# A scheduled attention and gated MLP kernel: first tile's x in two halves, four tiles gated by Silu, new priorities

## The chip, the cores and the metric

The kernel runs on one core of one Trainium2 chip. The core has five engines that work side by side, each through its own list of instructions in order: TensorE (PE, with its weight loads shown as PEld), VectorE (DVE), ScalarE (ACT), GpSimd (POOL) and SyncE (SP), which here only issues transfers. Sixteen DMA engines carry the transfers. The metric is device time in microseconds of one execution; the median of several runs is compared.

## What is computed

One sequence of 2048 tokens of width 448 is normalised. One branch is attention with 16 heads of width 28, in which a token sees eight tokens: itself and seven earlier ones, two apart. The other branch is an MLP of width 1792 with Gelu. The output is x plus the attention result times Silu of the MLP result. All arrays are bf16.

```python
xn = _layernorm(x)
q, k, v = split(xn @ wqkv)                     # 16 heads of 28
idx = pos[:, None] - 2 * arange(8)[None, :]    # masked where negative
s = (softmax(q . k[idx] * 28**-0.5) . v[idx]) @ wo
g = silu(gelu(xn @ w1 + b1) @ w2 + b2)
return x + s * g
```

## The kernel before

The tokens are split into even and odd ones, so that the dilated window becomes a plain window of eight neighbours; the 2048 positions are then cut into 16 tiles of 128 and 4 chunks of 512.

For each tile, `stats` (line 432) loads mean and variance with two DVE instructions (statistics, line 434, and aggregation, line 439), `rstds` (line 444) takes the square root on ACT and the reciprocal on DVE for the first four tiles (on POOL for the others), and `norm` (line 467) writes the normalised tile `xn` on DVE (line 469) and doubles its last 64 columns (line 474, POOL for the first four tiles). The first four tiles are transposed on PE (line 484) and copied to `xnT` (line 330 on DVE, 328 on ACT); the other twelve are transposed by DMA from SP (`dma_T`, line 389).

From `xnT` come three products. `qk_rows` (line 569) and `vproj` (line 592) give q, k and v of a tile; `first_batch` (line 542) does it for the first two tiles, weight part by weight part as the weights land, and `pair` (line 508) for two tiles or two outputs at a time, with the upper and the lower 64 rows of the array doing different work. q and k are copied to `qk_tok` and transposed by DMA to `qkT`; v goes to memory (`v_hbm`) and comes back as windows. `ff1` (line 645) gives the hidden layer, with Gelu on ACT (line 649), and `ff2` (line 677, for the last two tiles line 699) the MLP's output.

Attention goes in nine visits of up to 228 positions: scores on PE (line 744), exponential on ACT (line 753), mask on DVE (line 759), values on PE (line 773), and then on DVE two transposes, a reciprocal and a product (lines 782 to 796) that write `oT`. `final` (line 827) multiplies `oT` by wo (line 835, or 843 for the last two tiles).

The gate is in two functions. `gate` (line 712) takes the MLP output y, computes t = tanh(y/2) on ACT (line 723) and (t+1)y on DVE (line 727). `gated` (line 848) multiplies the attention result by half of that (line 850), adds x (line 856) and issues the output from SP (line 860). The last tile is cut into 336 and 112 columns (`parts`, line 660).

The order of the work is not written out. Every step is a task in `_Plan`: an engine (or several to choose from), an estimated cost, the tasks it needs, the buffers it takes and gives back, and a priority from the tables `PRIO` and `LATER`, moved by `NUDGE` for single tasks. `run` (line 99) walks through time by these estimates and, among the tasks of an engine that can start at about the same moment, takes the one with the highest priority. `emit` then writes each engine's instructions in that order. So a changed estimate or priority moves instructions on every engine, and at run time each engine follows its list and waits where an input is late.

A transfer (`dma`, line 369) is two tasks: the issue on SP, ACT or POOL, and a stretch on one modelled "DMA" engine with a rate and a tail until it has landed. At the start, x of tile 0 goes out from SP and x of tile 1 from ACT (lines 407 and 408), then from SP two of the three parts of wqkv, x of tiles 2 and 3 together, the third part and the two tails, then half of w1, x of tiles 4 to 7 and the other half. Until the first tile is there, PE runs warm-up matmuls on constants (line 343).

Of the kernel before, what the change touches and what calls it, by code (L numbers as in the profile page):

```python
# [10 lines left out]
ALU = mybir.AluOpType  # L11
# [164 lines left out]
def kernel(  # L176
# [82 lines left out]
    def ring(name, n, shape, dt=BF16, fifo=False):  # L259
# [24 lines left out]
        "project": (213.5, 84.5, 145, 57.5,),  # L284
        "project2": (61, 74.5, 113.5, -640,),
        "values": (199.5, -20, 128, 6,),
        "attn": (784, 1451, 452, 363, 27.5, 240.5, 361.5, 160.5, 204.5,),
        "ff1": (198.5, 215, 158, 71.5, 146.5, 194, 121, 197.5, 124, 116, 171.5, 143, 137, 144.5,
            114.5, 194, 150.5, 78.5, -21, 12, 47, 112.5, 51.5, 61.5, 93.5, 59.5, 175, 137,),
        "gelu": (5, 143.5, 52.5, 123.5,),  # L290
        "ff2": (805.5, -34.5, 231, 114.5, -2.5, 89, -623.5, 135, 208.5, 180.5, -39.5, 104, -4, 131,
            -80.5, -689,),
        "final": (-141.5, 2, -11, -16.5, 187, -2, 125, 203, -49.5, 65.5, -59.5, 162.5, -51, 134,
            6.5, 220.5,),
        "norm": (131, 11, 219.5, 294, 190, 208.5, 173, -1.5, 189, 173.5, 166.5, 159, 150.5, -11.5,
            127, 56,),
        "loads": (2.5, 106.5, -29, 61, -61,),
        "stats": (49, 32, 205.5, 205.5, 55, 91.5, -4.5, 56, 70.5, 178.5, 31, 101.5, -704, 2.5, 161,
            70.5,),
        "turn_x": (198, 4.5, 200, 12.5, 20.5, 38.5, 81, 163, 190.5, 214.5, 8.5, -3, 72, 153.5,  # L300
            72.5, 162.5,),
        "turn_qk": (-12.5, 15, 13, 198, 91, 58, -98.5, 69, 181.5, 168, 69.5, -36, 142, 100, 88,
            80.5,),
        "move_v": (19.5, -58, -99, 107.5, 62, 44, 64.5, 3, 68,),
        "store_v": (55.5, 68.5, -38.5, -16, 175.5, 53, 3.5, 13.5, 115.5, -7, 113, 144.5, 69, 170.5,
            147.5, 61.5,),
        "spread": (120, 175.5, 70.5, 58.5, 20, 222, 105.5, 24, 126,),
# [12 lines left out]
    def act(n):  # L320
        return 0.15 + n / 1130.0
# [19 lines left out]
    for i in range(48):  # L341
        def fn(k, n=512 if i < 10 else P):
            nc.tensor.matmul(buf(p_b, k)[:, :n], ones[:, :P], ones[:, :n], start=True, stop=True)  # L343
        t_warm = plan.add("PE", 0.427 if i < 10 else 0.107, fn, [t_warm], 1000 if i < 12 else -1000, take=(p_b,), limit=8.0)
        t_warm.give = ((p_b, t_warm, 0),)
# [23 lines left out]
    def dma(eng, dst, src, kb, prio, deps=(), issue=0.45, rate=350.0, tail=1.7):  # L369
# [5 lines left out]
        a = plan.add(eng, issue, fn, [t_on] + list(deps), prio)  # L375
        return plan.add("DMA", kb / rate, lambda _: None, [a], prio, tail=tail)
# [19 lines left out]
    def load_x(t0, n, prio, eng="SP", deps=()):  # L396
        d = dma(eng, x_sb[:, t0:t0 + n, :],
                rows(x_half, t0 * P, n * P).rearrange("(t p) d -> p t d", p=P), 112 * n, prio, deps,
                rate=250.0 if t0 < 2 * TPC else 230.0, tail=1.6 if t0 < 2 else 1.7)
        for t in range(t0, t0 + n):  # L400
            t_x[t] = d
# [5 lines left out]
    load_x(0, 1, 300, "SP")  # L407
    load_x(1, 1, 300, "ACT")
    t_w = []

    def load_w(kt, prio):
# [609 lines left out]
```

## Time and profile before

| What | Value |
|---|---|
| Median of 3 runs | 153.47 us (153.23 to 154.29) |
| The profiled execution | 153.43 us |
| Its span, from the first to the last instruction | 151.7 us |
| PE matmuls from the first warm-up to the last product | 0.84 to 147.68 us |
| HBM read and written | 9.42 MB and 3.94 MB |
| Table loads on ACT | 6, of 1.28 us each |

The profile shows one execution. "Busy" is the time in which an engine worked on an instruction; a share is of the span. The chain of work that ended last is followed back from the last instruction, at each step to what released it. A wait is put down to the event that came last. In a timeline, a row gives its start, its busy time, the engine and the line of the kernel, what is written and read, how many instructions are merged, and in brackets the idle time before it and what ended that. In the DMA issues, the last number is the time from issue to landing.

### The profile page before, as it was taken

The page shows a single profiled execution, that of the slowest core. Times are in us where ns is not written, and L with a number is a line of the kernel's source. Part 1 is how long each engine was busy: PE and PEld are TensorE (multiplying, and loading weights), DVE is VectorE, ACT ScalarE, POOL GpSimd, SP SyncE. Part 2 cuts the span into 40 slices and gives each one's busy share as a digit, 9 for nine tenths or more (in the row PEclk, how much of TensorE's full clock was granted, in tenths as well). Part 3 has the DMA queues.
Part 4 walks back from the last instruction along what each step waited for, and adds up shares of the span by engine and source line. Part 5 has one row for each costly group of instructions (what it writes and reads, how often), then busy time and mean ns, then how long its engine had stood idle before and what let it go on. Part 6 is the DMA issues. An engine that isn't in the chain of part 4 may idle for free.

```text
span 151.7 us, 5225 instructions
## 1 busy us (share of the span) xinstructions
PE 146.6 (97%) x2169; PEld 79.7 (53%) x2169; DVE 118.7 (78%) x288; ACT 90.5 (60%) x160; POOL 24.9 (16%) x62
## 2 busy tenths in 40 slices
PE   7999999999999999999999999999999999999990
PEld 2457555555567555556555554445566444554560
DVE  3786850624996997799998998889898978997972
ACT  3234969368796959658444457967396497602030
POOL 7435540100046900231201000000000000000000
PEclk9999999999999999999999999999999999999999
DMA  5999985499987973699945516222020000001221
GB/s 158 315 297 318 175 233 123 41 172 338 250 187 194 212 188 77 133 185 210 184 131 130 140 57 133 78 73 62 12 65 6 0 0 4 4 0 61 90 68 31
DMA packets 36983, 19.47 MB, mean 128 GB/s; under 512 B 24840, under 2 KB 35919, under 8 KB 36959
## 3 DMA queue, kind: packets, MB, share of 16 engines
q1 hardware_dynamic: 35774, 16.40, 47.4%
q0 software_dynamic: 1040, 2.62, 6.9%
q8 instruction: 17, 0.28, 0.7%
q10 hardware_dynamic: 144, 0.11, 0.3%
q14 instruction: 8, 0.06, 0.1%
HBM read 9.42 MB, written 3.94 MB: 88 GB/s over the span
## 4 chain that ended last, share of the span: by engine, by line
PE 95%; DVE 2%; ACT 0%; issue 0%; DVEq 0%; ACTq 0%
PE bank L645 28%; PE bank L677 25%; PE bank L569 14%; PE bank L592 7%; PE bank L835 7%; PE bank L773 4%; PE bank L699 3%; PE bank L343 3%; PE bank L744 2%; PE bank L484 1%; DVE sg L850 1%; DVE w_in L727 1%; PE bank L843 0%; DVE qk_tok L330 0%; ACT t L723 0%
## 5 line engine op out<-in xcount | busy, mean ns | idle before, releaser
L645 PE MATMUL bank<-xnT,w 64*128 64x512 bf16 x392 | 44.3, 376 | 0.0
L677 PE MATMUL bank<-w,h 64*128 64x448 bf16 x392 | 40.4, 349 | 0.0
L649 ACT ACTIVATE h<-bank,b 128x512 bf16<-128x512 f32 x56 | 34.0, 688 | 9.7 <-PE bank L645 9.3
L645 PEld LDWEIGHTS <-w 64*128 64x128 bf16 x392 | 20.4, 94 | 20.4
L677 PEld LDWEIGHTS <-h 64*128 64x128 bf16 x392 | 19.2, 94 | 16.0
L569 PE MATMUL bank<-w_in,xnT 64*128 64x448 bf16 (+1 forms) x212 | 25.1, 349 | 0.1
L753 ACT ACTIVATE E<-bank 128x456 bf16<-128x456 f32 (+1 forms) x36 | 16.8, 557 | 9.3 <-PE bank L744 9.3
L328 ACT CAST qk_tok<-bank 128x448 bf16<-128x448 f32 x23 | 11.5, 540 | 9.9 <-PE bank L569 8.5
L723 ACT ACTIVATE t<-y 128x448 f32<-128x448 f32 x15 | 8.6, 586 | 14.5 <-DVE y L717 14.5
L569 PEld LDWEIGHTS <-xnT 64*128 64x128 bf16 (+1 forms) x212 | 11.7, 94 | 9.4 <-DVE xnT L330 0.3
L782 DVE STREAM_TRANSPOSE dt<-bank 128x480 f32<-128x480 f32 (+1 forms) x18 | 12.1, 674 | 2.8 <-PE bank L773 2.8
L592 PE MATMUL bank<-w_in,xnT 64*128 64x448 bf16 (+1 forms) x106 | 13.5, 349 | 0.1
L791 DVE STREAM_TRANSPOSE dt<-rd 128x480 f32<-128x480 f32 (+1 forms) x18 | 12.1, 675 | 0.6
L835 PE MATMUL bank<-wo,oT 64*128 64x448 bf16 x112 | 12.4, 349 | 0.0
L434 DVE BATCH_NORM_STATS2 st<-x_sb 128x6 f32<-128x448 bf16 x16 | 9.6, 604 | 3.3 <-DMA x_sb<-in_A_x_dram 3.3
L759 DVE TENSOR_TENSOR E<-E,m_gen 128x456 bf16<-128x456 bf16 (+1 forms) x32 | 11.1, 387 | 1.3 <-ACT E L753 1.3
L796 DVE TENSOR_TENSOR oT<-bank,dt 128x456 bf16<-128x456 f32 (+1 forms) x18 | 11.4, 631 | 0.6
L330 DVE CAST qk_tok<-bank 128x448 bf16<-128x448 f32 x9 | 5.4, 618 | 7.8 <-ACT h L649 5.5
L717 DVE TENSOR_TENSOR y<-bank,b 128x448 f32<-128x448 f32 x15 | 8.9, 618 | 1.6 <-PE bank L677 1.6
L381 POOL DMA_DIRECT2D v_hbm<-v_tok x11 | 6.3, 572 | 21.3 <-PE bank L592 10.0
L592 PEld LDWEIGHTS <-xnT 64*128 64x128 bf16 (+1 forms) x106 | 6.0, 94 | 4.5 <-issue 0.3
L835 PEld LDWEIGHTS <-oT 64*128 64x128 bf16 x112 | 5.5, 94 | 5.1
(72 smaller groups left out, 143.7 us busy)
## 6 DMA issues: line engine op xcount, KB each, us to landing
out_dram<-o SPq DMA_DIRECT2D x15, 112.0 KB, 1.7
v<-v_hbm SPq DMA_DIRECT2D x13, 128.0 KB, 3.2
v_hbm<-v_tok POOLq DMA_DIRECT2D x11, 128.0 KB, 3.6
w<-in_B_w_dram SPq DMA_DIRECT2D x2, 672.0 KB, 7.5
x_sb<-in_A_x_dram SPq DMA_DIRECT2D x3, 448.0 KB, 6.9
w_in<-in_A_wqkv_dram SPq DMA_DIRECT2D x3, 336.0 KB, 4.4
w<-in_B_w_dram SPq DMA_DIRECT2D x2, 448.0 KB, 5.3
w<-in_B_w_dram SPq DMA_DIRECT2D x2, 336.0 KB, 6.5
```

The lines of the kernel that those rows point to most:

```text
L328: nc.scalar.copy(o, i)
L569: return nc.tensor.matmul(ps[:, :D], xnT[r, kt, cs], w, start=start, stop=stop)
L592: return nc.tensor.matmul(ps[:, :D], xnT[r, kt, k0:k0 + P], w, start=start, stop=stop)
L645: return nc.tensor.matmul(ps[:], w1[r, kt, ms], xnT[r, kt, cs], start=start, stop=stop)
L649: nc.scalar.activation(buf(p_h, own, i)[:], buf(p_b, own, i)[:], ACT.Gelu_apprx_tanh, bias=b1[:, mt:mt + 1])
L677: return nc.tensor.matmul(ps[:, :D], buf(*h_at[(c, mt)])[r, cs], w2[r, mt, :], start=start, stop=stop)
L753: nc.scalar.activation(buf(p_E, k)[:, :8 * n], buf(p_b, a, at + i)[:, :8 * n], ACT.Exp, scale=SCALE)
L759: nc.vector.tensor_tensor(out=E, in0=E, in1=m[:, :, :, :n].rearrange("p i g q -> p (i g) q"), op=ALU.mult)
L782: nc.vector.transpose(buf(p_dt, k)[:, :32 * m], buf(p_b, po, i)[:, :32 * m])
L791: nc.vector.transpose(buf(p_dt, d)[:, :32 * m].rearrange("p (b c) -> p b c", c=32), buf(p_rd, r)[:, :m].unsqueeze(2).to_broadcast((P, m, 32)))
L796: nc.vector.tensor_tensor(out=oT[:, a::2, q:q + 4 * n1], in0=buf(p_b, po, i)[:, :n].rearrange("p (l q) -> p l q", l=2), in1=buf(p_dt, d)[: ...
L835: return nc.tensor.matmul(ps[:, :D], oT[r, kt, t * P:(t + 1) * P], wo[r, kt, :], start=start, stop=stop)
```

## The change

There are four parts.

1. The start. Tile 0's x is loaded as two halves of 64 rows, one from SP and one from ACT; tile 1's x follows from ACT as a second issue. x of tiles 2 and 3 are two loads, the second behind the third part of wqkv. Loads without inputs are put in turn for the planner: on each issuing engine, and in their data. The planner's rates and tails of the transfers are new numbers. One of the ten long warm-up matmuls is now a short one.
2. Tile 0's norm stands ahead of tile 1's aggregation: `t_st[1]` gets it as an input.
3. The last four tiles (12 to 15) are gated by Silu on ACT, which writes the gate at once; the DVE step (t+1)y falls away for them, and `gated` multiplies without the factor one half. For the last tile, the sum may go to DVE or POOL and the output's issue to SP or ACT, as the planner chooses.
4. All priorities in `NUDGE`, `PRIO` and `LATER` are new, so that the planner gives a new order on every engine.

```diff
 NUDGE = {
-    82: 164, 83: 221, 88: -17, 98: 114, 148: -76, 155: 52, 210: 248, 309: -202, 522: -191, 633: 96,
-    635: 30, 656: -230, 898: 200, 985: 15,
+    76: -245, 137: -86, 141: -177, 146: -165, 158: -142, 176: 37, 178: -31, 263: -236, 298: 162, 301: 180,
...
-    LATER = {"swap": 102.5, "qk": -548.5, "v": 174.5, "gelu": 131.5, "exp": 44, "mask": -436, "pv": 158.5, "recip": 165.5, "os": 191, "y": 231, "tanh": -35.5, "g": 111.5, "sg": 40, "o": 208.5}
+    LATER = {"swap": 52.5, "qk": -1428, "v": -156.5, "gelu": 55.5, "exp": 90, "mask": -2112, "pv": 17, "recip": 91.5, "os": 93, "y": -7, "tanh": 127, "g": 168.5, "sg": 168.5, "o": 552.5}
...
-        def fn(k, n=512 if i < 10 else P):
+        def fn(k, n=512 if i < 9 else P):
...
-        a = plan.add(eng, issue, fn, [t_on] + list(deps), prio)
-        return plan.add("DMA", kb / rate, lambda _: None, [a], prio, tail=tail)
+        ahead = [] if deps else in_turn
+        a = plan.add(eng, issue, fn, [t_on] + list(deps) + [k for k, _ in ahead if k.eng == (eng,)][-1:], prio)
+        d = plan.add("DMA", kb / rate, lambda _: None, [a] + [k for _, k in ahead][-1:], prio, tail=tail)
+        if kb > 50 and not deps:
+            in_turn.append((a, d))
+        return d
...
-    load_x(0, 1, 300, "SP")
-    load_x(1, 1, 300, "ACT")
+    t_x[0] = [dma(e, x_sb[r:r + 64, 0, :], x_half[0, r:r + 64, :], 56, 300, rate=262.0, tail=1.4) for e, r in (("SP", 0), ("ACT", 64))]
+    load_x(1, 1, 299.5, "ACT", tail=1.4)
...
-    load_w(0, 299)
-    load_w(1, 298)
-    load_x(2, 2, 297, "SP")
-    load_w(2, 296)
+    load_w(0, 299, 0.85)
+    load_w(1, 298, 1.4)
+    load_x(2, 1, 297, "SP", tail=1.45)
+    load_w(2, 296, 1.45)
+    load_x(3, 1, 295.5, "SP", tail=1.4)
...
         a = plan.add("DVE", 0.40, f1, [t_rs[t]], prio if t >= TPC else 390 - t, take=(p_xn,))
+
+        if not t:
+            t_st[1].deps.append(a)
...
+        if t >= NT - TPC:
+            def f5(k):
+                nc.scalar.activation(buf(p_g, k)[:, :n], buf(pool, y, at)[:, :n], ACT.Silu)
+            t_g[t].append(plan.add("ACT", act(n), f5, after, prio + LATER["tanh"], take=(p_g,), give=held, table=("silu",)))
+            return
...
-            nc.vector.scalar_tensor_tensor(out=buf(p_sg, k)[:, :n], in0=buf(p_b, own, i)[:, :n], scalar=0.5,
-                                           in1=buf(p_g, g)[:, :n], op0=ALU.mult, op1=ALU.mult)
+            ps, by, o = buf(p_b, own, i)[:, :n], buf(p_g, g)[:, :n], buf(p_sg, k)[:, :n]
+            if t >= NT - TPC:
+                (nc.gpsimd if k.on == "POOL" else nc.vector).tensor_tensor(out=o, in0=ps, in1=by, op=ALU.mult)
+            else:
+                nc.vector.scalar_tensor_tensor(out=o, in0=ps, scalar=0.5, in1=by, op0=ALU.mult, op1=ALU.mult)
...
-        o = plan.add(("DVE", "POOL") if n == LAST else "DVE", (dve(n, 2), 0.1 + n * 0.0024) if n == LAST else dve(n, 2), f3, [s], prio + LATER["o"], take=(p_o,), give=((p_sg, s, 0),))
-
-        def f4(_):
-            nc.sync.dma_start(rows(o_half, t * P, P)[:, cs], buf(p_o, o)[:, :n])
-        q = plan.add("SP", 0.55, f4, [o], 50)
+        o = plan.add(("DVE", "POOL") if last else "DVE", (dve(n, 2), 0.1 + n * 0.0024) if last else dve(n, 2), f3, [s], prio + LATER["o"], take=(p_o,), give=((p_sg, s, 0),))
+
+        def f4(k):
+            (nc.scalar if k.on == "ACT" else nc.sync).dma_start(rows(o_half, t * P, P)[:, cs], buf(p_o, o)[:, :n])
+        q = plan.add(("SP", "ACT") if last else "SP", (0.35, 0.4) if last else 0.55, f4, [o], 50)
```

More of the change, by code (lines that the diff above doesn't have):

```diff
@@ L302 @@
[L302 to L307, printed above, removed]
+        "project": (110, 23, 95, 1.5,),
+        "project2": (61.5, 77.5, 2.5, -908.5,),
+        "values": (84, 64.5, 13, -255.5,),
@@ L435, in stats @@
         prio = PRIO["stats"][t] if t >= TPC else 380 - 2 * t
-        k = plan.add("DVE", 0.61, f1, [t_x[t]], prio, take=(p_st,))
+        k = plan.add("DVE", 0.63, f1, t_x[t], prio, take=(p_st,))
         def f2(_):
@@ L484, in f3 @@
                     nc.tensor.transpose(tp[:, kt, :], xn[:, kt * P:(kt + 1) * P], ident[:])
-            halves.append(plan.add("PE", 0.13 if t else 0.22, f3, [twice if i else a, t_ident] + halves, 400 - t, take=() if i else (p_b,),
-                                   give=((p_xn, a, 0),) if i else (), tail=0.15))
+            halves.append(plan.add("PE", 0.13 if t else 0.16, f3, [twice if i else a, t_ident] + halves, 400 - t, take=() if i else (p_b,),
+                                   give=((p_xn, a, 0),) if i else (), tail=0.12))
         b = halves[0]
@@ L720, in gate @@
         after = [a, y]
+        if t >= NT - TPC:
[3 more added lines that the diff above has]
+            return
         def f3(k):
             nc.scalar.activation(buf(p_t, k)[:, :n], buf(pool, y, at)[:, :n], ACT.Tanh, scale=0.5)
-        th = plan.add("ACT", act(n), f3, after, prio + LATER["tanh"], take=(p_t,), table=("exp", "gelu"))
+        th = plan.add("ACT", act(n), f3, after, prio + LATER["tanh"], take=(p_t,), table=("exp", "gelu", "silu"))
         def f4(k):
@@ L872, in load_w1 @@
         cs = slice(i * F // 2, (i + 1) * F // 2)
[L873 to L874 removed]
+        t_w1.append([dma("SP", w1[:, 0:3, cs], ktiles(B_w1[0:KF, cs]), 672, prio, deps, rate=262.0, tail=1.3)]
+                    + [dma("SP", w1[64 * i:64 * i + 64, 3, cs], B_w1[KF:D, cs], 112, prio, deps, rate=262.0, tail=1.3) for i in range(2)])
     load_w1(0, 91, [])
```

65 lines of the change are left out of this document (34 added, 31 removed), and 2 rows, old and new, of the table NUDGE.

## The prediction

> **What bounds the kernel now.** I read the busy shares and the chain of the page first, then the chain in order of time, then the timelines of the first 14 us and the last 14 us, and last the waits and the DMA issues. One execution is the yardstick throughout: the profiled one, 153.43 us with a span of 151.7, so 1.73 us lie around the span; the median of the runs, 153.47, is 0.04 above it.
>
> ```profile
> PE 146.6 (97%) x2169; PEld 79.7 (53%) x2169; DVE 118.7 (78%) x288; ACT 90.5 (60%) x160; POOL 24.9 (16%) x62
> ...
> PE 95%; DVE 2%; ACT 0%; issue 0%; DVEq 0%; ACTq 0%
> ```
>
> TensorE carries 95% of the chain. What is left to gain is small: the time before its first real matmul, its few waits, and the tail behind its last matmul.
>
> ```profile
> 6.11 0.30 DVE xnT L330
> 6.41 0.05 issue
> 6.46 0.36 PE bank L569
> ...
> 39.46 2.68 PE bank L569 x28
> 42.14 0.61 DVE qk_tok L330
> 42.76 0.04 issue
> 42.80 2.80 PE bank L592 x27
> ```
>
> In this chain, the first projection (L569) starts at 6.46, and one wait in the body shows: PE stands from 42.14 to 42.80 for a qk_tok copy, 0.66 us. To see the rest I sum the work by its rows: 392 ff1 matmuls x 0.108 (9.07 for 84) = 42.3; 392 ff2 x 0.0946 (2.65 for 28) = 37.1; q, k, v 300 x 0.0946 + 18 full ones x 0.189 = 31.8; wo 112 x 0.0946 = 10.6; nine score visits x 0.42 = 3.8; nine value visits x 0.72 = 6.5; the last two tiles 7.2; transposes 0.9. Together 140.2. From 6.46 to the end of the last matmul, 147.68, are 141.2 us. So PE loses 1.0 us there: 0.66 in that wait and 0.34 elsewhere, nearly all of it between 10.1 and 11.5, where tiles 2 and 3 come in.
>
> ```profile
> 3.35 0.63 DVE L434 BATCH_NORM_STATS2 st<-x_sb 128x6 f32<-128x448 bf16 x1 [1.43 <-DMA x_sb<-in_A_x_dram]
> 4.11 0.59 DVE L434 BATCH_NORM_STATS2 st<-x_sb 128x6 f32<-128x448 bf16 x1
> 5.00 0.40 DVE L469 TENSOR_SCALAR xn<-x_sb,mv,rstd 128x448 bf16<-128x448 bf16 x1
> 9.69 0.46 SPq L371 DMA_DIRECT2D v_hbm<-zero  x1
> ...
> 138.26 1.11 ACT L723 ACTIVATE t<-y 128x448 f32<-128x448 f32 x2 [6.26 <-DVE y L717]
> ...
> 146.28 0.45 ACT L723 ACTIVATE t<-bank 128x336 f32<-128x336 f32 x1 [1.62 <-PE bank L699]
> 146.76 0.76 DVE L727 SCALAR_TENSOR_TENSOR w_in<-t,bank 128x336 bf16<-128x336 f32 x2
> 147.62 0.28 DVE L850 SCALAR_TENSOR_TENSOR sg<-bank,w_in 128x112 bf16<-128x112 f32 x1
> 147.93 0.22 DVE L856 TENSOR_TENSOR o<-x_sb,sg 128x112 bf16<-128x112 bf16 x1
> 148.07 0.50 DVE L850 SCALAR_TENSOR_TENSOR sg<-bank,w_in 128x336 bf16<-128x336 f32 x1
> 148.60 0.33 DVE L856 TENSOR_TENSOR o<-x_sb,sg 128x336 bf16<-128x336 bf16 x1
> ```
>
> At the start, tile 0's statistics wait for its x until 3.35, tile 1's statistics (4.11) run ahead of tile 0's norm (5.00 to 5.40), and everything up to 6.46 follows from that norm: 1.06 us of transposes, the doubled columns on POOL, and the copy. At the end, DVE runs without a break from 146.76 to 148.93; PE is done at 147.68.
>
> ```profile
> x_sb<-in_A_x_dram ACTq DMA_DIRECT2D x1, 112.0 KB, 2.3
> x_sb<-in_A_x_dram SPq DMA_DIRECT2D x1, 112.0 KB, 2.5
> 2.00:3.00 1.00, 1.00 (x4) 0.37 (x3) 0.00 (x0) 0.69 (x2) 1.00 (x2) 1.00 1.00 312
> ```
>
> The two x tiles land 2.3 and 2.5 us after issue, side by side; the last number of the third line is what the DMA engines moved in that microsecond, 312 GB/s.
>
> **Start.** Today 224 KB are under way at once. With halves of tile 0 on both queues and tile 1 second on ACT's queue, 112 KB come first; 112 KB less at 312 GB/s is 0.36 us, so x lands near 2.95 instead of 3.30. Tile 1, issued one ACT issue (0.38) later, then lands at about 3.7 (336 KB ahead of or beside it, by the same rate), just as tile 0's statistics end (3.80). The order of the changed kernel has statistics 0, aggregation 0, statistics 1, reciprocal 0, norm 0, and only then aggregation 1. So norm 0 stands at 4.58 to 4.98, 0.42 earlier. What the added wait holds back is aggregation 1 and, behind the first xnT copy, norm 1, which ends near 6.6; PE wants it at 6.7, after three matmuls of tile 0, so it is covered by 0.1. If tile 1 lands at 4.2 (1.2 plus the 3.0 of the quickest w_in), statistics 1 block DVE and norm 0 gains 0.02. PE can take no more than 0.44: its warm-up (nine instead of ten of 0.427, then six short ones) ends at 5.01 instead of 5.45. I take 0.35 of the span 0.02 to 0.44, near the upper end since the rate row is the closest. The second issue on ACT stands ahead of its table load (1.28), which then ends at 2.9, before the first square root (3.9).
>
> **First batch.** Tile 3's x is now an issue of its own behind w_in's third part; SP issues eight loads for seven, so the tails go out 0.45 later and w1 and x 4 to 7 up to 0.6 later. The bytes ahead of the tails are the same. The v_hbm issue at 9.69 waited 0.9 us for the last of them, so they land at about 9.65; PE, 0.35 earlier, wants them at 9.6: 0 to 0.1 of wait. Norm 3 ends near 10.45 by its chain (x3 at about 8.4, then statistics, root, reciprocal, norm), and PE wants it at 10.5. Of today's 0.34 us I let 0.1 go (ends 0 and 0.34).
>
> **The body.** The new priorities reorder all engines, but the work on PE is the same except for one warm-up. What changes is who waits. The wait at 42.14 belongs to the old order: scores there follow the projections whose copies were behind eight statistics on DVE. In the new order 28 ff2 matmuls (2.65 us) stand ahead of the first scores and 56 and 14 behind: minus 0.66. Against it, I put PE's new order beside DVE's and ACT's by the rows from 48 to 92 us: six hand-overs have less than 0.3 us to spare (copies of q and k before the fourth scores, oT before three ff2 or wo groups, the exponentials before the third value visit, oT before chunk 2's first ff1). Each costs between nothing and 0.66, the longest wait of this kind in the trace; I take 0.4 for all six (ends 0 and 1.2). DVE's load there, 25.3 us of rows in 28 us, is no higher than now (27 us from 64 to 91 with under 1 idle), so it does not become the bound.
>
> **Silu and the tail.** Four tiles lose the tanh and the (t+1)y step: five DVE instructions, 0.62 x 3 + 0.50 + 0.27 = 2.6 us, go. ACT gets Silu for tanh, and a seventh table load. No Silu is in the trace; I take tanh's rows (0.58 and 0.45; the Gelu's 0.69 for 512 columns is the upper end, hardly more per column). The load stands behind the last Gelu with no wait, in the 6.26 us in which ACT was idle; without that cover it costs 1.28. Behind the last tile, sg 112 waits for its Silu (146.95 + 0.26 = 147.21) instead of two DVE steps (147.53), and the last four steps start 0.3 earlier, until sg 336 meets the end of PE. I take 0.27 (ends 0.2 and 0.30). Both last outputs stay on SP in the order built, so their 1.4 and 1.6 us are as now.
>
> **Sum.** -0.35 - 0.10 - 0.66 + 0.40 - 0.27 = -0.98: 153.43 becomes 152.45; with the 0.04 to the median, 152.5 us.
>
> **A rule weighed.** The row first: x of tile 0 takes 2.5 us beside tile 1's. The Trainium skill, DMA: Bandwidth & Descriptors (Rules for kernel authors), says of two transfers to disjoint partition halves not to bother, since both spread over the same 16 engines. By that the halves bring nothing in themselves, and what I count comes from tile 1's bytes moving behind; the sum by the rule alone is that of the third case below. The nearest row speaks for a gain, as the two tiles landed at nearly the same time though issued from two queues.
>
> **The rivals.** Clean: the first batch and the hand-overs cost nothing. -0.44 - 0.34 - 0.66 - 0.30 = -1.74: 151.7. For it speaks that the old order has one visible wait in 90 us; against it the six narrow places.
>
> No earlier start: halves and tile 1 get in each other's way, norm 0 stays near 5.00, the batch too. -0.66 + 0.40 - 0.27 = -0.53: 152.9.
>
> Slower, by the transposed x of tiles 4 to 7: today four of them go out in a row from 19.81, 1.25 us each, and land 2.6 us later. In the new SP order two more v_hbm stores and a qkT transpose stand ahead of the last two, and the stores wait for ACT copies behind the first two Gelus. By the rows (qkT 1.34, 2.06, 2.62) the third leaves at 24.1 and lands at 26.7; PE wants it at 27.5. From 0.8 us of slip PE waits, and from 1.8 the kernel is slower than before. A landing of 5.0, the longest of xnT, gives +1.6: 154.1; three qkT at the longest row, 3.56, give +4.6 - 0.8: 156.3. Against it: the landings at that time were 2.5 to 3.6.
>
> A later clock: PE's 512-column matmuls ran at 0.427 until about 4.7, 3.9 us after its start, and at twice the rate after. With one warm-up less the rise may come 3.9 us later, at 8.6; 2.5 us of the first batch would run at half rate, +1.25: 153.7. The Trainium skill, TensorE: Matmul & The Clock Gate (What's actually happening), ties the rise to time, a window of about 3.4 us, and not to a count of matmuls; the one profile agrees, and so the lost warm-up should not matter.
>
> **How the numbers follow.** Forecast 0.50, clean 0.22, no earlier start 0.13, late transposes 0.10, later clock 0.05. Within 1%, which a measurement of this kernel can about tell from no change, is 151.9 to 155.0. Faster: the clean case, 0.22. Slower: half of the late transposes, 0.05. Same: 0.73. The range 151.6 to 154.2 takes in all but the late transposes and the edge of the clean case.
>
> **What would show it.** First L569 (now at another line) near 6.1 and norm 0 ahead of aggregation 1; statistics 0 near 3.0. No wait of PE before the first scores. PE's last matmul near 147.0 and DVE's last step about 0.98 behind it. Seven table loads, the last ahead of 138. I am wrong if PE waits for xnT near 27, if the hand-overs from 62 to 92 cost over 1 us, or if statistics 0 still start at 3.3.

## The result, and the profile after

The changed kernel takes 161.94 us (median of four runs, 159.84 to 163.5) against 153.47: slower, the ratio is 1.050 with an interval of 1.039 to 1.061. The forecast was 152.5, the range 151.6 to 154.2. The profiled execution below is the slowest of the four, 163.5 us with a span of 161.8; the kernel before has a span of 151.7. Of the experiments, medians and ranges are given over all runs of a kernel, while ratios leave out runs over 1.5% above its fastest.

The busy shares, the slices of TensorE and its granted clock, and the chain, from the page of the changed kernel:

```profile
PE 149.5 (92%) x2168; PEld 77.1 (48%) x2168; DVE 112.5 (70%) x274; ACT 98.4 (61%) x170; POOL 22.6 (14%) x58
...
PE   7999999999809999999999967999999999999990
...
PEclk9999999999965999999999999999999999999999
...
PE 75%; DMA 12%; DVE 5%; SPq 3%; ACT 2%; issue 1%; POOL 0%; POOLq 0%; DVEq 0%; ACTq 0%
```

TensorE fell from 95% of the chain to 75%, and DMA transfers now hold 12%; one load of x alone holds 7% of the span. One slice is empty (the 0, near 46), and in it and the next one the clock row reads 6 and 5. Another dent is at 93 to 101 (6, 7). The chain in order of time around the empty slice:

```profile
33.46 11.05 DMA x_sb<-in_A_x_dram
44.51 0.02 issue
44.54 0.64 DVE st L442
...
47.45 0.19 DVE mv L447
47.64 0.09 issue
47.73 0.30 POOL sd L464
48.04 0.04 issue
48.08 0.03 POOLq L536
48.11 0.05 issue
48.15 1.46 PE bank L656 x6
49.62 1.49 PE bank L580 x8
51.11 1.28 PE bank L656 x6
52.39 0.88 PE bank L580 x6
```

Read it upwards from L656. TensorE waits for L536, the "tell" in the middle of a row-halves pair: an empty instruction on another engine's queue that releases the second half. This tell had nothing to wait for any more, but it stands on GpSimd's queue behind the variance step of tiles 8 to 11 (L464), that behind VectorE's statistics, and those behind the load of x of tiles 12 to 15. In the new order on SP that load is issued at 33.46, behind all four parts of w2 (before: at 31.0, ahead of three of them), and lands 11.05 us later.

The four groups behind the wait take 5.11 us; the same four groups take 2.73 in a run without a low clock (shown with the kernel "filled" below). The wait itself is 4.30. The second dent, as VectorE's timeline and SP's have it:

```profile
92.65 0.49 DVE L642 TENSOR_SCALAR kd<-qkT,head 128x1024 bf16<-128x1024 bf16 x1 [2.40 <-DMA qkT<-qk_tok]
...
95.49 0.39 DVE L878 TENSOR_TENSOR o<-x_sb,sg 128x448 bf16<-128x448 bf16 x1 [0.86 <-DMA out_dram<-o]
```

```profile
82.56 8.89 SPq L396 DMA_TRANSPOSE qkT<-qk_tok  x3
91.50 0.58 SPq L388 DMA_DIRECT2D v_hbm<-v_tok  x1
92.18 0.37 SPq L882 DMA_DIRECT2D out_dram<-o  x1
```

Three transposes hold SP for 8.89 us, the output stores stand behind them, and VectorE waits first for a transpose and then for a free o buffer; TensorE has 2.3 us of idle time in the 20 us from 80 to 100 (17.70 busy), in three waits for VectorE:

```profile
93.72 0.40 PE L761 MATMUL bank<-qkT,kd 64*128 64x57 bf16 x17 [0.68 <-DVE sg L873]
94.68 0.37 PE L761 MATMUL bank<-qkT,kd 64*128 64x57 bf16 x15 [0.56 <-DVE sg L873]
...
98.19 2.07 PE L580 MATMUL bank<-w_in,xnT 64*128 64x448 bf16 x20 [1.05 <-DVE oT L813]
```

At the start, statistics 0 begin at 3.29 (before 3.35), norm 0 at 4.91 (5.00). The eight matmuls behind the first batch, before and after:

```profile
11.42 1.03 PE L569 MATMUL bank<-w_in,xnT 64*128 64x448 bf16 x8
```

```profile
11.88 0.93 PE L580 MATMUL bank<-w_in,xnT 64*128 64x448 bf16 x8
```

So the start that should have gained 0.35 has lost 0.46 by then, between these two executions. The row of before is an early one: in two later executions with the old start untouched (before with Silu, and before with the late load) the eight start at 11.78 and 11.81. The tail:

```profile
154.89 0.39 DVE L878 TENSOR_TENSOR o<-x_sb,sg 128x448 bf16<-128x448 bf16 x1 [0.93 <-DMA out_dram<-o]
155.20 0.62 DVE L728 TENSOR_TENSOR y<-bank,b 128x448 f32<-128x448 f32 x1
156.46 0.62 DVE L871 TENSOR_TENSOR sg<-bank,w_in 128x448 bf16<-128x448 f32 x1 [0.64 <-ACT w_in L735]
...
157.55 0.28 DVE L871 TENSOR_TENSOR sg<-bank,w_in 128x112 bf16<-128x112 f32 x1
```

VectorE ends 1.37 us behind TensorE (158.86 against 157.49), before 1.25: here tile 14's y (L728) stands behind a step that waits 0.93 for an output buffer, and pushes back the last tile's steps. Before has such a wait too (0.60 at 144.59), but there tile 14's y, at 143.37, stands ahead of it.

The bill at TensorE's last matmul (157.49, before 147.68): 4.30 of wait, 2.4 of low clock, 2.3 near 90, 0.46 at the start, less the old wait of 0.66 at 42.14, which is gone: 8.8 of the 9.8 us. The last 1.0 us I have not placed.

### The profile page after: what moved, and what is told of

It reads as the page before. It is cut to its first block, busy times and chain, and to the rows that moved or that the text cites. A ratio compares the mean times of both kernels' runs of the same rounds, so it can differ in the third digit from the quotient of the medians.

```text
span 161.8 us, 5226 instructions
## 1 busy us (share of the span) xinstructions
PE 149.5 (92%) x2168; PEld 77.1 (48%) x2168; DVE 112.5 (70%) x274; ACT 98.4 (61%) x170; POOL 22.6 (14%) x58
## 4 chain that ended last, share of the span: by engine, by line
PE 75%; DMA 12%; DVE 5%; SPq 3%; ACT 2%; issue 1%; POOL 0%; POOLq 0%; DVEq 0%; ACTq 0%
PE bank L688 21%; PE bank L656 19%; PE bank L580 11%; DMA x_sb<-in_A_x_dram 7%; PE bank L852 6%; PE bank L603 5%; PE bank L710 3%; PE bank L790 3%; PE bank L344 3%; DMA xnT<-xn 3%; PE bank L761 2%; DMA out_dram<-o 2%; SPq L372 2%; DVE st L442 1%; ACT h L660 1%
## 5 line engine op out<-in xcount | busy, mean ns | idle before, releaser
L656 PE MATMUL bank<-xnT,w 64*128 64x512 bf16 x392 | 47.5, 384 | 4.3 <-POOLq L536 4.3
L660 ACT ACTIVATE h<-bank,b 128x512 bf16<-128x512 f32 x56 | 34.5, 688 | 16.0 <-PE bank L656 15.6
L656 PEld LDWEIGHTS <-w 64*128 64x128 bf16 x392 | 19.5, 95 | 27.1 <-POOLq L536 4.7
L580 PE MATMUL bank<-w_in,xnT 64*128 64x448 bf16 (+1 forms) x212 | 26.7, 362 | 1.4 <-DVE oT L813 1.1
L688 PEld LDWEIGHTS <-h 64*128 64x128 bf16 x392 | 18.6, 94 | 16.4 <-issue 0.2
L580 PEld LDWEIGHTS <-xnT 64*128 64x128 bf16 (+1 forms) x212 | 10.9, 98 | 11.9 <-issue 3.1
L603 PE MATMUL bank<-w_in,xnT 64*128 64x448 bf16 (+1 forms) x106 | 14.0, 349 | 0.0
L640 ACT ACTIVATE kd<-qkT,head 128x1024 bf16<-128x1024 bf16 x9 | 10.0, 1153 | 0.6 <-DMA qkT<-qk_tok 0.6
L388 POOL DMA_DIRECT2D v<-v_hbm x7 | 4.5, 639 | 38.1 <-PE bank L603 15.4
L728 DVE TENSOR_TENSOR y<-bank,b 128x448 f32<-128x448 f32 x15 | 8.8, 617 | 1.4 <-PE bank L688 1.4
L735 ACT ACTIVATE w_in<-y 128x448 bf16<-128x448 f32 x3 | 1.7, 577 | 11.6 <-DVE y L728 11.6
L329 ACT CAST v_tok<-bank 128x448 bf16<-128x448 f32 x15 | 7.4, 534 | 2.0 <-PE bank L603 2.0
```

Of the source, the lines that this page charges most:

```text
L329: nc.scalar.copy(o, i)
L580: return nc.tensor.matmul(ps[:, :D], xnT[r, kt, cs], w, start=start, stop=stop)
L603: return nc.tensor.matmul(ps[:, :D], xnT[r, kt, k0:k0 + P], w, start=start, stop=stop)
L656: return nc.tensor.matmul(ps[:], w1[r, kt, ms], xnT[r, kt, cs], start=start, stop=stop)
L660: nc.scalar.activation(buf(p_h, own, i)[:], buf(p_b, own, i)[:], ACT.Gelu_apprx_tanh, bias=b1[:, mt:mt + 1])
L688: return nc.tensor.matmul(ps[:, :D], buf(*h_at[(c, mt)])[r, cs], w2[r, mt, :], start=start, stop=stop)
```

## Experiments

Eleven kernels keep the changed kernel's order of instructions, and seven (the late load, the code parts, the start's parts) keep that of the kernel before; only the tasks named are moved in it (the numbers are the tasks' places in the program; `ahead(a, b, c)` puts b and c ahead of a). In the expectations, STT is VectorE's scalar_tensor_tensor instruction, and sg the product of gate and attention result. Theory 1 is the reading above: a tell behind late work on GpSimd, and a low clock behind the idle time. The rivals are the late loads as such, and the start or the tail.

**x of tiles 12 to 15 first.**

```diff
+    ahead(304, 300, 301)   # 300: load of x 12-15; 304: first part of w2 on SP
```

> One DMA issue of the changed kernel is moved on SP's queue: the load of x of tiles 12 to 15 goes ahead of w2's four parts (right behind x of tiles 8 to 11), as in the kernel before; nothing else. Theory 1 (GpSimd's queue): the late x holds the variance step of tiles 8 to 11 on GpSimd, the tell of a row-halves pair stands behind it, TensorE idles 4.3 us and then runs some 5 us at half clock (about 2.3 us lost). So x lands near 38, the idle time at L656 goes, and the time falls by 6 to 7 us to about 155.3 (154.5 to 156.3). Theory 2 (the loads as such, DMA throughput: only the order in which things come late is changed): w2's parts land later by what x lands earlier, TensorE waits for w2 at L688 instead, and the time stays above 159. Theory 3 (the new start or the tail is what costs): stays near 161.9.

Measured: 157.87 (154.09 to 160.86). The median fits neither theory. Three of seven runs are at 154.1 to 154.7, at or below the lower end of theory 1; the wait at L656 is gone in the trace. The profiled run, 160.41, shows why the others are not:

```profile
55.98 0.69 PE L790 MATMUL bank<-E,v 64*32 64x57 bf16 x64 [1.85 <-DVE y L728]
56.60 4.50 PE L688 MATMUL bank<-w,h 64*128 64x448 bf16 x28
```

A norm on VectorE waited 2.0 us for a free xn buffer (a transpose of x still under way), the masks stood behind it, TensorE waited 1.85, and again its clock fell: 28 matmuls in 4.50 instead of 2.81. The granted clock is 1.00 until 57.1, 1.1 us after the matmuls resume, and 0.50 from there to 60.5. So the load's place was the cause at L656, and the same kind of row lies in wait 8 us later.

**Statistics of tiles 12 to 15 later, loads untouched.**

```diff
+    ahead(455, 329, 330, 335, 336, 331, 332, 333, 334, 337)   # 329-336: statistics 12-15; 337: their variance step; 455: norm 15
```

> The changed kernel with its loads untouched (x of tiles 12 to 15 still lands near 44.5), but the statistics and the variance step of tiles 12 to 15 are put behind the norms of tiles 8 to 11 on VectorE and behind the waiting tells on GpSimd. Theory 1 (GpSimd's queue): the variance step of tiles 8 to 11 no longer waits for that x, the idle time at L656 goes with no byte landing earlier: about 155.3 (154.5 to 156.5). Theory 2 (late loads as such): still above 159, the wait only moves to a later reader of tiles 12 to 15. The two kernels, this and the one with x earlier, agree within 1 us by theory 1.

Measured: 156.28 (156.05 to 157.72). The load has its old place and lands near 43.7 (44.5 in the changed kernel's trace), and 5.7 us are back: the late load as such is not what costs. Between the two profiled executions it is 7.45 us; the wait, its low clock and the dent near 90 (4.30, 2.4 and 2.3), which this execution does not have, less the new wait of 1.65 make 7.35. The rest is one wait on the next tell, again behind a variance step on GpSimd; the clock stays at 1.0:

```profile
51.30 2.82 PE L688 MATMUL bank<-w,h 64*128 64x448 bf16 x28 [1.65 <-POOLq L536]
```

**Three tells on SP's queue.**

```diff
+    for i in (566, 571, 252):
+        plan.tasks[i].on = "SP"
```

> The changed kernel with three instructions moved: the tells of the two feed-forward pairs and of the query/key pair that stand behind the waiting variance step on GpSimd's queue are issued on SP's queue, which the profile shows idle there. Loads, statistics, variance steps and norms stay as late as they were. Theory 1: TensorE no longer waits 4.3 us at L656 and keeps its clock; what is left is that the norms of tiles 8 to 11 come 6 us late and hold VectorE's copies of query/key: 155.3 if that is covered, up to 158 if those copies hold TensorE's banks. Theory 2 (the late x itself is what stops TensorE, the tell only shows it): TensorE waits as long one or two groups later, and the time stays above 160.

Measured: 163.3 (159.34 to 166.27): the change does not help. The wait at L656 shrinks to 0.43, but the third tell now stands on SP behind transposes of x that wait for the late norms:

```profile
44.48 0.82 PE L656 MATMUL bank<-xnT,w 64*128 64x512 bf16 x6 [0.43 <-SPq L536]
...
50.28 1.30 PE L580 MATMUL bank<-w_in,xnT 64*128 64x448 bf16 x6 [3.57 <-SPq L536]
```

GpSimd is not special: SP's in-order queue with late work does it too. My narrower expectation (the covered case) was wrong; that the wait reappears a group later is what the rival said, but its reason, the missing data, is refuted by the run before.

**The wait filled with work.** Eighteen extra matmuls, their result thrown away.

```diff
+        for _ in range(18):
+            nc.tensor.matmul(p_b.bufs[7][:], ones[:, :P], ones[:], start=True, stop=True)
         swap(k)   # task 567, the second half that waits
```

> The changed kernel with 18 extra matmuls of 512 columns on constants (3.8 us of work whose result is thrown away) put on TensorE just ahead of the pair that waits 4.3 us at L656, so that the wait is filled with work and the wait's cause is left as it is. If the low clock behind the stall comes from TensorE's idleness: groups behind it run at their usual durations (six matmuls of L656 in 0.65 us, not 1.46), the granted clock stays near 1.0, and the time falls by 2 to 2.5 us to about 159.6. If the low clock has another cause (it comes with the DMA traffic or the time of the run): no change, 161.9, or longer by what the extra work overruns the wait.

Measured: 158.24 (158.22 to 160.39), 3.7 us less than the changed kernel though 18 matmuls are added and the wait's cause is left. The chain:

```profile
42.69 1.32 PE bank L688 x14
44.02 4.04 PE bank L1015 x18
48.06 0.75 PE bank L656 x6
48.81 0.76 PE bank L580 x8
49.57 0.65 PE bank L656 x6
50.22 0.57 PE bank L580 x6
```

The four groups behind take 2.73 us and not 5.11: the low clock comes from the idle time. Between the two profiled executions 5.3 us are gone: 2.4 by the clock, 2.3 with the dent near 90, which this one does not have. Here x landed some 2 us earlier (its first statistics at 42.60, not 44.54), so by my estimate the tell was free near 46.2, and the extra matmuls, up to 48.06, overran the wait. The changed kernel's profile is its slowest run, and its wait of 4.30 need not be the usual one. The Trainium skill, TensorE: Matmul & The Clock Gate (Why this matters for your kernels), says that gaps without matmuls over about 3 us put the clock back to half; by that rule the 4.3 us do, and the trace agrees. The 1.85 us with x first lie below that figure, and the clock fell all the same: there the trace differs from the rule. The 1.65 us with the statistics later left the clock alone.

**Both repairs; then the old start, then Tanh, put back on top.**

```diff
+    ahead(304, 300, 301)
+    ahead(455, 329, 330, 335, 336, 331, 332, 333, 334, 337)
```

> The two repairs together in the changed kernel: x of tiles 12 to 15 loaded ahead of w2, and the statistics and variance step of tiles 12 to 15 behind the norms of tiles 8 to 11. Theory 1 (the tells behind a late variance step on GpSimd, and the low clock behind the idle time, are the whole loss): no wait of TensorE on a tell over 0.3 us, granted clock 1.0 throughout, and 154.3 (153.6 to 154.8), the same within 1% as before; the profile after the repairs then shows what start and tail are really worth. Rival (part of the loss lies elsewhere: the transposes and output stores in one row on SP's queue near 82 to 98 in the changed kernel, where VectorE waited 2.4 us): 156 to 157.5 with idle time of TensorE near 90.

Measured: 155.87 (155.7 to 158.35). The 1.6 us on the next tell is still there, since the second edit also puts that variance step late; x was early for nothing. Neither 154.3 nor the rival's idle time near 90 in the profile (20.00 busy of 20); two of six runs are at 158.3, and no profile shows what holds them.

```diff
+    plan.tasks[65].fn = lambda _: nc.sync.dma_start(x_sb[:, 0, :], rows(x_half, 0, P))
...
+    ahead(92, 94, 95)
+    ahead(136, 96, 138)
+    ahead(100, 101, 102, 103)
```

> As the kernel with both repairs, but with the start of the kernel before: x of tile 0 whole on SP's queue, x of tiles 2 and 3 in one load, statistics of tile 1 ahead of norm 0 and those of tile 3 ahead of norm 2, both copies of tile 0 on VectorE. If the new start was worth 0.35 us, as the prediction had it: 0.3 to 0.4 us slower than with both repairs. If the new start costs what the trace shows (the eight matmuls behind the first batch start at 11.95 and not 11.48): 0.4 to 0.5 us faster.

Measured: 158.24 (156.17 to 159.23), but the eight matmuls stand at 11.98 against 11.88, and 1.7 of the 2.3 us between the two profiles are idle time near 90 (18.32 busy of 20). So this kernel says of the start only that the old loads do not bring the half microsecond back.

```diff
-                nc.scalar.activation(buf(p_g, k)[:, :n], buf(pool, y, at)[:, :n], ACT.Silu)
+                nc.scalar.activation(tt, by, ACT.Tanh, scale=0.5)
+                nc.vector.scalar_tensor_tensor(out=buf(p_g, k)[:, :n], in0=tt, scalar=1.0, in1=by, op0=ALU.add, op1=ALU.mult)
```

> As the kernel with both repairs, but the last four tiles are gated as before: Tanh on ScalarE and the STT that builds g on VectorE, sg with factor 0.5; the scratch of Tanh lies in w1, which is dead by then. If Silu and the tail were worth 0.27 us, as the prediction had it: 0.2 to 0.4 us slower than with both repairs. If the tail gained nothing (the trace of the changed kernel has VectorE 1.37 us behind TensorE's last matmul, before 1.25): no difference, within 0.15.

Measured: 157.67 (157.37 to 160.04), 1.8 slower: VectorE then ends 3.0 us behind TensorE, not 1.2. In this order Silu is worth far more than 0.27, since the added steps stand ahead of the last ones; in the old order it is less (below).

**The late load in the kernel before.**

```diff
+    for i in (296, 297):          # load of x 12-15
+        plan.order.remove(plan.tasks[i])
+    at = plan.order.index(plan.tasks[303 - 1]) + 1   # behind w2's last part
+    plan.order[at:at] = [plan.tasks[296], plan.tasks[297]]
```

> The kernel BEFORE with one DMA issue moved: the load of x of tiles 12 to 15 goes behind w2's last part on SP's queue, as in the changed kernel; every other instruction is where it was. Theory 1: in this order too, two statistics of that x stand ahead of the last statistics of tiles 8 to 11 on VectorE, and tells stand behind their variance step on GpSimd, so TensorE stalls 2 to 5 us between 42 and 50 and its clock drops: 156 to 161. Theory 3 (the load's place is harmless, and the loss needs the new start, the narrow hand-overs or Silu): 153.5, no change.

Measured: 158.2 (156.96 to 159.82), ratio 1.027 (1.024 to 1.031). One DMA issue moved makes the old kernel slower by 4.7 us (158.2 against 153.53 beside it).

```profile
46.53 4.34 PE L592 MATMUL bank<-w_in,xnT 64*128 64x448 bf16 x27 [3.43 <-DVE qk_tok L330]
```

The size is as expected, the path is not: here it is not a tell, but a qk_tok copy on VectorE that stands behind statistics waiting 3.56 us for x; the 27 matmuls take 4.34 instead of 2.80. The clock is 1.00 through the wait and falls at 47.6, 1.1 us after the matmuls resume, to 0.50 until 51.0.

**More rows cleared.** Statistics 8 to 11 first, norms 15 and 12 behind the masks; then transposes of query/key ahead of loads of v; then tile 2's transposes earlier; then statistics 3 earlier.

```diff
+    ahead(304, 300, 301)
+    ahead(385, 329, 330, 335, 336, 331, 332, 333, 334)
+    ahead(580, 455, 456, 443, 444, 445, 446, 457, 458)
```

> The changed kernel with x of tiles 12 to 15 loaded ahead of w2, all statistics of tiles 8 to 11 ahead of those of tiles 12 to 15 on VectorE (GpSimd's order as it was), and the norms of tiles 15 and 12, which waited for free xn buffers 3.0 and 2.0 us near 50, put behind the four masks they held up. Theory 1 (tells and masks behind late work in an in-order queue, and the low clock behind the idle time): no wait at L656, none on a tell at L688 and none at L790; 154.3 in every run that does not stall near 90 (153.9 to 154.7), that is the level of the best three runs with x first (154.09 to 154.68). If the remaining wait of 1.6 us at L688, seen with both repairs, has another cause: 155.8 again.

Measured: 155.19 (153.76 to 157.39), ratio 1.009 (1.005 to 1.013); no wait on a tell is left, and three of eight runs, the best, are near the level of before (153.76 to 154.46). But "none at L790" is missed: VectorE's y stands behind a norm that still waits 1.17 for a free xn buffer, and TensorE waits 0.84. The profiled run, 157.39, has that and the dent near 90:

```profile
54.88 0.69 PE L790 MATMUL bank<-E,v 64*32 64x57 bf16 x64 [0.84 <-DVE y L728]
...
87.21 0.49 DVE L642 TENSOR_SCALAR kd<-qkT,head 128x1024 bf16<-128x1024 bf16 x1 [2.76 <-DMA qkT<-qk_tok]
```

```diff
+    ahead(435, 424, 464)
```

> As the kernel clean, with two transposes of query/key (qkT of the third group) issued on SP ahead of two loads of v that wait for their stores. If the stall near 90 (VectorE's kd waiting 2.4 us for qkT, in some runs only) comes from this place in SP's row: the slow runs, some 2.4 us above the best, disappear and the median is 154.3 or below. If it comes from the transfers taking 8.8 instead of 4.9 us whatever their place: slow runs stay as frequent as in clean.

Measured: 155.14 (154.1 to 155.69). No run is above 156, where clean had two of eight, and in the trace the wait of 2.76 is gone; but the median is not lower, and in the next two kernels, which keep this edit, two of six and four of twelve runs are above 156 again. So such runs are about as frequent as in clean, and SP's row is not shown to make the dent. The level of 155.1 is placed in the main: of the 2.2 us by which this span exceeds before's (153.9 against 151.7), 0.78 are the late first batch (the eight at 12.20, not 11.42), 0.71 a wait at L790 and 0.2 one for xnT.

```diff
+    ahead(179, 146, 147)
```

> As clean_qkT, with the two transposes of tile 2 on TensorE put ahead of the first two of the batch's row-halves groups, where they are in the kernel before (there at 9.85, here at 10.44). If the half microsecond lost in the first batch comes from this order: the eight matmuls behind the batch start near 11.45, not 11.88, and the time falls by 0.4 us. If it comes from x of tile 3 by itself (norm 3 at 10.17, before 9.46): they start at 11.8 or later and nothing is won.

Measured: 155.61 (153.72 to 156.49), and the eight matmuls start at 11.97: above 11.8, so by the expectation nothing is won. Executions of one start differ by as much (11.42 to 11.81 with the old one, 11.88 to 12.20 in this order), so a gain of some 0.2 could hide. In the profiled run, 156.21, TensorE waits 1.19 for oT at 91.17.

```diff
+    ahead(100, 101, 102, 103)
```

> As clean_turn, and the statistics of tile 3 on VectorE ahead of norm 2, as in the kernel before. If norm 3 (10.17) holds the batch: norm 3 near 9.5 and another 0.2 to 0.4 us won. If the transposes' place was the whole loss: no change within 0.15; norm 2 comes 0.7 us later and may even cost that.

Measured: 154.58 (153.69 to 158.03), ratio 1.005 (1.003 to 1.008); the eight start at 12.14, again no gain at the start. The scatter hides a few tenths.

**The code parts in the old order.** The kernel before, whose 29 runs beside these lie between 153.05 and 153.92, with the new start, with Silu, and with both.

```diff
+    plan.tasks[65].fn = lambda _: nc.sync.dma_start(x_sb[:64, 0, :], rows(x_half, 0, 64))
+    plan.tasks[67].fn, plan.tasks[75].fn = f_x1, f_w2
+    plan.tasks[73].fn = lambda _: part(2, nc.sync)
+    ahead(92, 90, 91)
+    plan.tasks[133].on = "ACT"
```

> The kernel BEFORE with the new start alone, every other instruction where it was: x of tile 0 in halves by SP and ScalarE, x of tiles 2 and 3 in two loads with w's third part between them, norm 0 ahead of the statistics' second step of tile 1, the second copy of tile 0 on ScalarE. The prediction priced this start at 0.35 us gained. The changed kernel's trace had statistics 0 at 3.29 against 3.35, so by the trace: 0.1 us gained at most, and within 0.3 of before in any case: 153.1 to 153.8.

Measured: 153.89 (153.55 to 156.46), ratio 1.0030 (1.0015 to 1.0045): 0.3 to 0.5 slower, where 0.35 was to be gained, and above the 153.8 that I expected at most.

```diff
+                nc.scalar.activation(w1[:, t % 4, cs], buf(pool, y, at)[:, :n], ACT.Silu)
...
+                nc.vector.tensor_tensor(out=buf(p_sg, k)[:, :n], in0=buf(p_b, own, i)[:, :n], in1=w1[:, t % 4, cs], op=ALU.mult)
```

> The kernel BEFORE with the gate of the last four tiles by Silu, in the old order: Silu on ScalarE in Tanh's place, the STT that built g left out, sg a plain product; Silu's result lies in w1, dead by then. The prediction priced this at 0.27 us gained at the tail (153.2). If the tail is bound by VectorE behind the last matmul, more is won than that, since two narrow STTs of 0.76 us in sum stand ahead of the last sg on VectorE: 152.7 to 153.0. If TensorE's last matmul bounds it: 153.4.

Measured: 152.95 (152.69 to 153.18), ratio 0.9964 (0.9949 to 0.9978): 0.55 us faster by the ratio, and no kernel of this study is faster. The table load lies in ScalarE's idle time, and the first sg of the last tile waits for Silu. VectorE ends 0.91 us behind TensorE, before 1.25, so 0.34 of the gain is seen at the tail:

```profile
132.00 1.28 ACT L724 ACT_TABLE_LOAD   x1
138.18 1.11 ACT L724 ACTIVATE w<-y 128x448 bf16<-128x448 f32 x2 [4.90 <-DVE y L717]
...
147.22 0.28 DVE L856 TENSOR_TENSOR sg<-bank,w 128x112 bf16<-128x112 f32 x1 [0.63 <-ACT w L724]
```

> The kernel BEFORE with both code parts, the new start and Silu, in the old order of the rest. The sum of the two alone: 152.6 to 153.3; by the prediction's two prices 153.5 less 0.62, 152.9. With this no tell stands behind late x, so nothing like the changed kernel's 162: if it did come out over 155, the code parts and not the new order would be the cause of the loss.

Measured: 153.33 (153.16 to 156.09), ratio 0.9994 (0.9979 to 1.0009). The code of the change, both parts together, costs nothing: the loss is the new order's.

In this kernel the edits of the two before it stand together; the change's one shorter warm-up matmul is not in it.

**The start's three parts, one at a time on Silu.** Halves first, f_x1 issuing the other half ahead of tile 1 on ScalarE's queue:

```diff
+    plan.tasks[65].fn = lambda _: nc.sync.dma_start(x_sb[:64, 0, :], rows(x_half, 0, 64))
+    plan.tasks[67].fn = f_x1
```

> The kernel before with Silu (its own runs: 152.95), and x of tile 0 in halves by SP and ScalarE; x of tiles 2 and 3 in one load and VectorE's order as before. By the prediction's working (112 KB first at 312 GB/s) statistics 0 start near 3.0 and the time falls by 0.2 to 0.35: 152.6 to 152.75. By the traces of the changed kernel and of the new start in the old order (statistics 0 at 3.29 and 3.45, before 3.35): no gain, 152.9 to 153.2.

Then tile 3's x behind w's third part (f_w2 issues both):

```diff
+    plan.tasks[75].fn = f_w2
+    plan.tasks[73].fn = lambda _: part(2)
```

> The kernel before with Silu (152.95), and x of tiles 2 and 3 in two loads, tile 3's behind w's third part on SP; nothing else of the new start. The trace of the whole new start in the old order has statistics 3 waiting 0.28 for its x, statistics 2 at 7.92 (before 7.30) and the first batch's end 0.6 late (12.04 against 11.42). If the late x of tile 3 is the cost of the start: 153.2 to 153.5. If the order of VectorE is: 152.95.

Then norm 0 ahead of aggregation 1 and of tile 1's root, and the copy on ScalarE:

```diff
+    ahead(92, 90, 91)
+    plan.tasks[133].on = "ACT"
```

> The kernel before with Silu (152.95), and norm 0 ahead of the second statistics step of tile 1 with tile 0's second copy on ScalarE; loads as before. If this order is what costs (norm 1 ends at 6.40 and not 5.91 in the trace of the new start, and statistics 2 stand behind it): 153.2 to 153.5. If it wins what it was priced at for norm 0 alone (some 0.1 us earlier): 152.85.

Measured, against 152.95 with Silu alone: 152.95, 153.02 and 153.36 (the ratios to before are 0.9965, 0.9960 and 0.9991, with Silu alone 0.9964). Halves and the later x are worth nothing either way; the third edit, norm 0 ahead together with the copy on ScalarE, costs 0.4. VectorE's timeline with it:

```profile
3.32 0.63 DVE L434 BATCH_NORM_STATS2 st<-x_sb 128x6 f32<-128x448 bf16 x1 [1.40 <-DMA x_sb<-in_A_x_dram]
...
4.79 0.40 DVE L469 TENSOR_SCALAR xn<-x_sb,mv,rstd 128x448 bf16<-128x448 bf16 x1
5.10 0.18 DVE L439 BATCH_NORM_AGGREGATE mv<-st 128x2 f32<-128x6 f32 x1
5.64 0.16 DVE L450 RECIPROCAL rstd<-sd 128x1 f32<-128x1 f32 x1 [0.36 <-ACT sd L447]
5.84 0.40 DVE L469 TENSOR_SCALAR xn<-x_sb,mv,rstd 128x448 bf16<-128x448 bf16 x1
```

From statistics 0, norm 0 comes 1.47 us later (1.66 with Silu alone, 5.16 less 3.50), but norm 1 comes 2.52 later and not 2.16: aggregation 1 now stands behind norm 0, and VectorE waits for ScalarE's root. Norm 0 gains 0.19, norm 1 loses 0.36, and the batch ends 0.28 later by the clock, 0.46 later from statistics 0 (the eight matmuls at 12.06 against 11.78).

The wait that TensorE shows, though, is for the copy on ScalarE. With Silu alone:

```profile
6.65 0.37 ACT L328 COPY xnT<-bank 128x256 bf16<-128x256 bf16 x1 [1.25 <-PE bank L484]
7.08 0.27 PE L484 MATMUL bank<-ident,xn 128*128 128x128 bf16 x2
```

With the third edit:

```profile
6.66 0.65 ACT L328 COPY xnT<-bank 128x256 bf16<-128x256 bf16 x2 [1.05 <-DVE xnT L330]
7.35 0.27 PE L484 MATMUL bank<-ident,xn 128*128 128x128 bf16 x2 [0.31 <-ACT xnT L328]
```

ScalarE has two copies in a row where it had one, and TensorE's next transposes start 0.27 later; both kernels with the whole new start in the old order show the same wait of 0.31. So the 0.28 by the clock go with the copy, and norm 1's lateness at most uses up the 0.18 by which x was earlier. No run separates the two.

## Why the prediction was wrong

**The body is the step that failed.** It said: "I put PE's new order beside DVE's and ACT's by the rows from 48 to 92 us: six hand-overs", 0.4 us in sum with an upper end of 1.2. Two engines were left out of that comparison, GpSimd and SP, and so were the loads from 30 to 48. TensorE lost 4.30 us in one wait, ended at 48.15, on a queue that the step does not name, and 2.4 more by the low clock behind it. All three links stand in the program's order: w2's four parts ahead of this x on SP, two statistics of this x ahead of the last ones of tiles 8 to 11 on VectorE, the tell behind their variance step on GpSimd. The gain of 0.66 was real: that wait is gone. The hand-overs that the step did name cost nothing when the dent stays away (with both repairs TensorE is busy for 20.00 of the 20 us from 80 to 100), and 2.3 us with it.

**Its upper end.** Each hand-over was bounded by 0.66, the longest such wait in the trace of before. A wait on an in-order queue is as long as what stands ahead of it is late, and no row of a smooth trace bounds that.

**The clock.** The rival looked for it in the warm-up; the clock rose on time (the first projections take 0.19 us each, as before), and fell at 46.1 instead, in the idle time that I did not see. It multiplied the wait: 4.30 became 6.7.

**Start.** -0.35 was wrong in sign. "112 KB less at 312 GB/s is 0.36 us, so x lands near 2.95": it started statistics 0 at 3.29 against 3.35, and the halves alone measure 152.95 against 152.95. ScalarE's second issue, priced at 0.38, ended with the first at 1.97 (1.17 for both), and the table load at 3.28, not 2.9. The rule weighed there (the Trainium skill, DMA: Bandwidth & Descriptors, Rules for kernel authors: for two halves, don't bother) was right, and I counted against it. The 0.4 us which the kernels with one part of the start each show come with norm 0 ahead and the copy on ScalarE. Norm 1 was priced too early ("near 6.6", it ended at 6.82), and the copy was not priced at all, though in the old order the traces have TensorE's wait there.

**First batch.** -0.10 was to come from x of tile 3 as a load of its own; in the old order it is worth nothing (153.02 against 152.95). In the new order the batch lost 0.46 in the two profiles, less against other executions of the old start; what of that is the third edit's and what the other order's is not separated, as neither repair there (11.97 and 12.14) brought it back.

**Silu and the tail.** -0.27 has the right sign; in the old order it measures -0.55, of which the traces show 0.34 at the tail and leave 0.2 open. In the new order the tail of this execution shows none of it, as tile 14's y stood behind a step that waited 0.93 for an output buffer.

**The rivals.** None of the four is what happened. No wait for xnT showed near 27. Rightly listed was what would make me wrong: statistics 0 near 3.3, and it was; and hand-overs costing over 1 us in the work up to 92, which is the dent of 2.3 here, some 7 us later behind the wait at 48.

Open: some 1.0 us of the profile's difference, some 0.5 us of the level of the cleared kernels, and why the transposes near 82 land in some 5 us in some executions and in over 8 in others (medians from 70 to 95: 4.3 with both repairs, 8.4 in the first cleared kernel). That the DMA engines are busy there is seen (shares of 1.40, 0.67, 1.29 and 1.07 in the four windows of 4 us from 70 on, in the first cleared kernel); that it is the cause was only argued.

## What to carry to other kernels

Before pricing a new order, follow every in-order queue, GpSimd's and SP's included, and ask of each short instruction that releases another engine what stands ahead of it and what that waits for; a load moved behind others is priced at its last reader's whole row. Where TensorE may idle for some two us, add what a halved clock takes behind it. A step pulled forward is paid for by the one it passes, and a copy moved to another engine by what then stands behind it: count both tiles and both engines.

## What the runs showed that I had not expected

- The clock fell behind idle times of TensorE of 4.30 us (four groups in 5.11 us, full rate 2.73) and also of 1.85 us (28 matmuls in 4.50, full rate 2.81), but not behind one of 1.65 us. It fell 2.2 us into the idle time in the changed kernel, and 1.1 us after the matmuls had resumed in two others; it stayed low for 6.8 us there (46.1 to 52.9) and for 3.4 us here (57.1 to 60.5, 47.6 to 51.0). Matmuls on constants in the gap kept it up.
- One moved load of 448 KB cost the old kernel 4.7 us, and the changed kernel's runs reach over 3.7 us where before's reach over 1.1: an order with little slack is not only slower, it scatters.
- In two halves by two queues, the half on ScalarE's queue took 0.55 us to issue, tile 1's x behind it 0.59, and ScalarE's table load moved from 1.21 to 2.00; x was there no earlier.
